# Another written order for a kernel's opening, with products of a zeroed tile and a first weight piece in three parts

## The chip, the core and the metric

The kernel runs on one core of a Trainium2 chip. The metric is device time in microseconds (us) from one launch, and lower is better. A core has TensorE (PE; its weight loads are listed apart, as PEld), VectorE (DVE), ScalarE (ACT), GpSimd (POOL) and SyncE (SP), whose queue issues all DMAs of this kernel. Each engine works through its own instructions in the order in which they stand in the program, and waits there for what the next one needs.

## What is computed

The reference, cut to what matters:

```python
# q, k, v: (4, 8, 576, 64), float32
out_d  = softmax-attention of q, k, v averaged over groups of 4 positions, repeated 4 times
out_l  = softmax-attention over |i - j| < 4 alone
x      = (out_d + out_l) as (2304, 512)
a, b   = x @ w1, x @ w2            # (512, 1024) each
h      = ((a * b) @ w3) @ w_out    # w3 (1024, 1024), w_out (1024, 512)
h2     = h @ w_in                  # (512, 2048)
out    = (h2 * sigmoid(h2)) @ w_out2   # (2048, 512)
```

The arrays come as 64-bit floats and are turned into 32-bit ones on the chip.

## The kernel before

The work is done in three stages that overlap at their edges.

**The opening** is everything up to the first tokens' products with w1 and w2. Three kinds of work are mixed in it. Attention is done in units (one batch and one pair of heads; 16 in all, numbered 0 to 15; the opening does units 0 to 4 and the first part of unit 5). The weights w3 and w_out are multiplied with each other beforehand, so that w3 and w_out need only one product with the tokens later: 64 products of 128x512, named `p` half, pair, number (`p000` to `p137`), on pieces of w3 (names `t`) and w_out (names `o`). And the pieces of w1 and w2 (`w12_0` to `w12_7`) are loaded and turned into a high and a low part. Every piece of a weight goes through a load in two halves (`L...0`, `L...1`), a scaling on ScalarE (`a...`) and three steps on VectorE (`d1`, `d2`, `d3`); a piece of w12 has two more steps (`h` on ScalarE, `l` on VectorE).

In a unit, `Lq`, `Lr`, `Lva`, `Lvb` are its loads; `s` and `sd` the scores on TensorE, `mk`, `ml`, `md`, `rd`, `rl` their masks, maxima and inverse sums on VectorE, `x..` and `n..` exponentials and scalings on ScalarE, `td`, `tl` transposes on TensorE with `cd`, `cl` their copies on ScalarE, `od`, `ol` the sums on TensorE, `pq`, `pv`, `os`, `xf`, `xo` further steps on VectorE, `xh` on ScalarE. `ab` are the products with w1 and w2.

**What sets the order.** The string `OPENING` names every step of the opening, and the program is made by going through it once, so that each engine's order is that of the names that are its own:

```python
    with tc.manual_schedule(engines={T.PE, T.DVE, T.Activation, T.Pool, T.SP}):
        for name in OPENING:
            ops.pop(name)()
```

**Buffers.** The first weight pieces in `KEYS` are loaded into memory lent by later stages (numbers 0 to 3 and 6 to 9 of the list); numbers 4, 5 and all from 10 on share two staging buffers of one tag (`stage(stg, "st")`), so that a load waits until the piece whose buffer it takes has been through its `d3`. Transposes and sums of attention share two PSUM banks, scores two, all 128x512 products four.

**After the opening** the groups `ab`, `y` and the remaining attention units run in slots. `bg_load(n)` loads the 16 pieces of the last two weights in the background, into the same two staging buffers. Then the last stage (`h_unit`, `out_block`) makes the products with w_in and w_out2.

Of the kernel before, what the change touches and what calls it, by code (L numbers as in the profile page):

```python
# [34 lines left out]


OPENING = """
Lwo00 Lwo01 Lq0 Lwt000 Lwt001 Lr0 Lwt010 Lwt011 Lwo10 ao0a d2o0a d1o0a Lwo11 d3o0a ao0b d2o0b
d1o0b d3o0b Lva0 s0 pq0 Lvb0 at00a d2t00a sd0 mk0 ml0 Lq1 at00b d1t00a x00 Lwo20 d3t00a d1t00b
x10 p000 md0 Lwo21 x20 p001 d2t00b d3t00b p002 Lq2 xd0 pv00 rl0 p003 pv10 at01 d2t01 Lwt020 p004  # L40
rd0 n00 d1t01 p005 Lr1 nd0 d3t01 Lwt021 p006 Lwt030 n10 d2o1 td00 n20 td10 p007 cd00 Lwt031 pq1
cd10 tl00 ao1 s1 Lwt100 tl10 cl00 sd1 d1o1 cl10 Lwt101 d3o1 ao2 tl20 od0 cl20 md1 Lwo30 p010 os0
xd1 mk1 p011 ml1 Lq3 ol0 pq2 x01 Lwo31 x11 p012 rd1 pv01 Lwt110 pv11 sd2 nd1 d1o2 d2o2 x21 Lva1
s2 d3o2 p013 at02 Lr2 p014 rl1 d2t02 n01 p015 d1t02 Lvb1 n11 p016 d3t02 n21 Lwt111 p017 d2t03
p020 d2t10 at03 Lww12_30 xf00 p021 xf10 xh00 d1t03 td01 xh10 Lww12_31 td11 d3t03 cd01 p022 cd11
Lwt120 xo00 tl01 ao3 tl11 xo10 p023 d2o3 cl01 Lwt121 d1o3 cl11 p024 Lq4 d3o3 tl21 od1 cl21 md2
p025 os1 p026 xd2 mk2 d2t11 ol1 ml2 rd2 pq3 x02 p027 Lva2 Lvb2 nd2 p030 d2w12_3 sd3 xf01 at10
xf11 pv02 td02 aw12_3 d1t10 td12 s3 d3t10 xh01 xh11 p031 Lq5 x12 d1w12_3 p032 d3w12_3 x22 p033
cd02 d2t12 p034 Lww12_60 hw12_3 Lww12_61 xo01 p035 xo11 wh00 lw12_3 cd12 p036 wh01 wl00 p037
wh02 wl01 p100 wh03 wl02 at11 p101 rl2 wl03 p102 pv12 n02 d1t11 Lr3 aw12_6 p103 d3t11 p104 n12  # L50
d1w12_6 n22 p105 d2w12_6 tl02 d3w12_6 tl12 cl02 p106 cl12 pq4 Lwt130 tl22 od2 Lwt131 cl22 pv03
p107 os2 pv13 p110 at12 md3 Lr4 ol2 mk3 xd3 ml3 d1t12 p111 x03 Lva3 d3t12 Lvb3 sd4 x13 d2t13 s4
Lww12_40 x23 Lww12_41 rd3 xf02 p112 Lq6 nd3 xf12 rl3 p113 md4 n03 pq5 td03 n13 td13 p114 cd03
pv04 cd13 p115 n23 p116 xh02 d2w12_4 aw12_4 tl03 xo02 tl13 cl03 p117 d1w12_4 cl13 xh12 tl23
d3w12_4 xd4 od3 p120 xo12 hw12_6 Lww12_00 os3 p121 Lww12_01 rd4 mk4 hw12_4 lw12_6 p122 at13 p123
lw12_4 cl23 p124 nd4 d1t13 ol3 d3t13 p125 ml4 aw12_0 Lww12_10 d2w12_0 Lww12_11 p126 Lva4 x04
xf03 Lvb4 p127 d1w12_0 xh03 d3w12_0 p130 x14 p131 xo03 x24 Lww12_20 xf13 Lww12_21 p132 pv14
hw12_0 rl4 Lr5 p133 xh13 d2w12_1 aw12_1 p134 lw12_0 p135 n04 d1w12_1 wh10 p136 wh11 d3w12_1 p137
n14 wh12 wl10 td04 Lww12_70 wh13 td14 wl11 Lww12_71 hw12_1 ab000a wl12 ab000b wl13 aw12_2 ab000c
lw12_1 ab001a af00 ab001b n24 d1w12_2 ab001c cd04 d2w12_2 ab010a cd14 cf00 ab010b cc00 ab010c  # L60
aw12_7 d3w12_2 co00 ab011a af01 ab011b xo13 Lww12_50 hw12_2 d1w12_7 ab011c Lww12_51 tl04 d2w12_7
tl14 cl04 sd5 cf01 cl14 cc01 lw12_2 tl24 co01 od4 cl24 s5 d3w12_7 ab020a Lq7 os4 ab020b hw12_7
md5 ab020c mk5 aw12_5 ab021a lw12_7 ab021b af02 ab021c ml5 xd5 ab030a d1w12_5 ab030b x05 cf02
ab030c cc02 x15 rd5 ab031a d2w12_5 co02 ab031b d3w12_5 af03 ab031c nd5 ab040a cf03 x25 ab040b
cc03 ab040c co03 hw12_5 rl5 ab041a ab041b af04 lw12_5 n05 ab041c ol4 n15 cf04 n25 cc04 ab050a
co04 Lva5 xf04 ab050b xf14 Lvb5 xh04 ab050c xh14 xo04 ab051a af05 xo14 ab051b ab051c ab060a cf05
ab060b cc05 ab060c co05 ab061a af06 ab061b ab061c ab070a cf06 ab070b cc06 ab070c co06 ab071a
af07 ab071b ab071c ab100a cf07 ab100b cc07 ab100c co07 ab101a af10 ab101b ab101c cf10 cc10 co10
""".split()


# [1067 lines left out]
```

## Time and profile before

| | |
|---|---|
| median of 3 runs | 860.12 us (859.17 to 861.5) |
| the profiled execution's own time | 860.39 us |
| its span, first to last instruction | 858.6 us |
| TensorE busy | 832.3 us, 97% of the span |
| VectorE, ScalarE, GpSimd busy | 490.9, 304.8, 266.0 us |
| mean granted TensorE clock | 0.995 |

The profile is of one execution. Busy time of TensorE counts a product from its start to its modelled end, so a busy TensorE need not be one at full speed. A time without a name in what follows is counted from the span's start. A product with 32-bit operands has two records.

### The profile page before, as it was taken

What the parts mean: (1) busy time and instruction counts of PE and PEld (TensorE: products, weight loads), DVE (VectorE), ACT (ScalarE), POOL (GpSimd) and SP (SyncE); (2) the same over time, 40 slices, a digit from 0 to 9 for tenths busy, and PEclk for the clock granted to TensorE, in tenths of its full rate; (3) what the DMA queues carried; (4) which work ended last, traced back from release to release, by engine and by line L of the source; (5) the groups of instructions that cost most, each with busy time, mean ns of one, the idle gap of its engine ahead of it and who ended that gap; (6) DMA issues with size and microseconds to landing.
All of it is one profiled execution on the core that took longest, in us unless ns stands there. A gap on an engine that the chain in (4) does not pass through costs nothing.

```text
span 858.6 us, 17384 instructions
## 1 busy us (share of the span) xinstructions
PE 832.3 (97%) x7104; PEld 738.1 (86%) x7104; DVE 490.9 (57%) x831; ACT 304.8 (36%) x880; POOL 266.0 (31%) x214
## 2 busy tenths in 40 slices
PE   5999999999999999999999999999999999999996
PEld 3544688999999999999999899899998999989985
DVE  6898984476564746446954444446544447534433
ACT  5777854454434553543322111122211123211111
POOL 3000132353533545131443133235232434222210
PEclk9999999999999999999999999999999999999999
DMA  9976663364546462426960675362662432822403
GB/s 322 347 250 195 202 201 99 126 223 158 206 139 220 152 212 82 179 89 237 349 269 23 251 264 214 134 220 87 178 227 86 129 128 86 235 97 99 158 2 74
DMA packets 39728, 149.16 MB, mean 174 GB/s; under 512 B 4448, under 2 KB 11616, under 8 KB 33504
## 3 DMA queue, kind: packets, MB, share of 16 engines
q1 hardware_dynamic: 39648, 148.05, 50.8%
q8 instruction: 56, 0.92, 0.4%
q14 instruction: 24, 0.20, 0.1%
HBM read 115.52 MB, written 32.51 MB: 172 GB/s over the span
## 4 chain that ended last, share of the span: by engine, by line
PE 88%; DVE 5%; DMA 4%; ACT 1%; issue 1%; SPq 0%
PE o L957 23%; PE ab L619 23%; PE h L1033 20%; PE y L684 12%; PE wp L571 3%; DMA st<-w 2%; PE ol L456 2%; DMA qk<-qk 1%; PE tl L404 1%; PE sd L332 1%; PE td L382 1%; PE s L357 1%; PE od L434 1%; ACT band L304 1%; DMA lent<-wo 0%
## 5 line engine op out<-in xcount | busy, mean ns | idle before, releaser
L957 PE MATMUL o<-wo,g 128*128 128x512 f32 x864 | 221.4, 393 | 0.0
L957 PEld LDWEIGHTS o<-wo,g 128*128 128x128 f32 x864 | 160.7, 188 | 25.3
L1004 POOL TENSOR_TENSOR g<-sg,g 128x768 fp32r<-128x768 f32 x46 | 84.9, 1845 | 250.1 <-DVE g L1002 242.3
L1033 PE MATMUL h<-yc,wcb 128*128 128x384 f32 x576 | 116.1, 337 | 0.0
L684 PE MATMUL y<-c,w_wC 128*128 128x320 f32 (+1 forms) x768 | 111.1, 301 | 0.0
L619 PE MATMUL ab<-x,w_wB 128*128 128x320 f32 (+1 forms) x768 | 108.9, 296 | 1.3 <-DVE w_wB L249 1.3
L1033 PEld LDWEIGHTS h<-yc,wcb 128*128 128x128 f32 x576 | 103.3, 188 | 7.7
L659 POOL TENSOR_TENSOR c<-cf,c 128x320 fp32r<-128x320 f32 (+1 forms) x64 | 74.1, 1158 | 107.2 <-DVE c L654 102.4
L619 PE MATMUL ab<-x,w_wA 128*128 128x320 f32 (+1 forms) x768 | 106.2, 296 | 0.1
L684 PEld LDWEIGHTS y<-c,w_wC 128*128 128x128 f32 x768 | 104.2, 191 | 1.3 <-issue 1.0
L619 PEld LDWEIGHTS ab<-x,w_wB 128*128 128x128 f32 x768 | 102.2, 188 | 2.6 <-DVE w_wB L249 1.6
L619 PEld LDWEIGHTS ab<-x,w_wA 128*128 128x128 f32 x768 | 102.1, 188 | 0.9 <-DVE w_wA L249 0.3
L996 ACT ACTIVATE sg<-cf 128x768 f32<-128x768 f32 x24 | 20.3, 847 | 184.7 <-DVE cf L1021 184.7
L1033 PE MATMUL h<-yc,wca 128*128 128x384 f32 x432 | 83.4, 336 | 1.4 <-DVE cg L1021 1.4
L1033 PEld LDWEIGHTS h<-yc,wca 128*128 128x128 f32 x432 | 76.5, 188 | 5.5 <-DVE cg L1021 1.7
L635 DVE TENSOR_TENSOR cf<-ab,af 128x320 f32<-128x320 f32 (+1 forms) x64 | 29.0, 454 | 63.7 <-PE ab L619 51.5
L571 PE MATMUL wp<-w_wo,w_w 128*128 128x512 f32 x128 | 62.9, 634 | 0.9 <-DVE w_w L178 0.9
L418 POOL TENSOR_TENSOR vr<-vr 72x512 f32<-72x512 f32 x11 | 15.7, 1432 | 118.3 <-DMA vr<-vr 118.2
L996 ACT ACTIVATE sg<-cg 128x768 f32<-128x768 f32 x24 | 20.3, 847 | 88.4 <-DVE cg L1021 88.4
L1021 DVE TENSOR_TENSOR u<-h,u 128x384 f32<-128x384 f32 x48 | 26.6, 553 | 40.1 <-PE h L1033 39.9
L571 PEld LDWEIGHTS wp<-w_wo,w_w 128*128 128x128 f32 x128 | 24.2, 201 | 26.9 <-issue 23.7
L304 ACT ACTIVATE band<-band,sml 128x38 f32<-128x38 f32 x144 | 45.0, 318 | 5.5 <-DVE sml L373 2.9
(111 smaller groups left out, 991.8 us busy)
## 6 DMA issues: line engine op xcount, KB each, us to landing
wcb<-wsd SPq DMA_DIRECT2D x24, 1024.0 KB
wca<-wsd SPq DMA_DIRECT2D x24, 768.0 KB
sw<-wb SPq DMA_DIRECT2D x32, 512.0 KB
qk<-qk SPq DMA_DIRECT2D x16, 579.0 KB
st<-w SPq DMA_DIRECT2D x16, 512.0 KB
wsd<-res SPq DMA_DIRECT2D x8, 1024.0 KB
wod<-res SPq DMA_DIRECT2D x8, 1024.0 KB
wo<-wod SPq DMA_DIRECT2D x8, 1024.0 KB
```

The costliest lines, as they stand in the source:

```text
L304: nc.scalar.activation(E[:, j, :], src[:, j, :], AF.Exp, bias=z[:, j:j + 1], scale=scale, accum_out=z[:, NQB + j:NQB + j + 1],)
L456: nc.tensor.matmul(acc[h][r, c0:c0 + QW], lhsT=v[k, sub, c, r], rhs=ET[k, c, q0:q0 + QW], start=True, stop=True,)
L571: nc.tensor.matmul(wp_ps[half, j], lhsT=w3v[:, k, j * P:(j + 1) * P], rhs=wov[:, k, :], start=(gp == 0 and k == 0), stop=(gp == 3 and k == 1),
L619: nc.tensor.matmul(acc[:, :N], lhsT=wv[:, i, w, kk, :], rhs=X[b, h, kk][:, j, :], start=(n == 0), stop=(n == 11),)
L635: nc.vector.tensor_tensor(out=cf, in0=C.pop(("ab", b, h, m, 1))[:, :N], in1=C.pop(("af", b, h, m)), op=ALU.mult)
L659: mark(nc.gpsimd.tensor_tensor(out=c[:, 1], in0=C.pop(("cf", b, h, m)), in1=c[:, 0].bitcast(F32), op=ALU.subtract))
L684: nc.tensor.matmul(acc[:, :N], lhsT=WP[kf // 2][:, i, kf % 2, ec * P:(ec + 1) * P], rhs=c[:, j, :], start=(kf == 0 and n == 0), stop=(kf = ...
L957: nc.tensor.matmul(acc, lhsT=g[:, a, j * P:(j + 1) * P], rhs=w[:, b, half, :], start=(p == 0 and half == 0 and n == 0), stop=(p == 7 and h ...
L996: nc.scalar.activation(sg, c, AF.Sigmoid)
L1004: e.tensor_tensor(out=g[:, 1], in0=sg, in1=g[:, 0].bitcast(F32), op=ALU.subtract)
L1021: nc.vector.tensor_tensor(out=out_, in0=in0, in1=in1, op=op)
L1033: nc.tensor.matmul(acc, lhsT=wc[w][:, a, c, kt * P:(kt + 1) * P], rhs=y[:, b, kt, :], start=(n == 0), stop=(n == 5),)
```

## The change

The order in `OPENING` is another one throughout, and so is the list `KEYS`: the first piece of w3 is now loaded and decoded ahead of the first of w_out, in three parts instead of two (256, 256 and 512 columns), and the pieces of w12 come in the order 0, 2, 3, 1, 5, 4, 6, 7 instead of 3, 6, 4, 0, 1, 2, 7, 5. A zeroed tile of 128x320 is made by VectorE; nine products of 128 of its columns with 288 of its columns stand at the very start of TensorE's program, and two more (`z0`, `z1`) behind `sd0`; nothing reads their result. `bg_load(1)` is planned six slots later.

```diff
@@
+NWARM = 9
@@
 OPENING = """
-Lwo00 Lwo01 Lq0 Lwt000 Lwt001 Lr0 Lwt010 Lwt011 Lwo10 ao0a d2o0a d1o0a Lwo11 d3o0a ao0b d2o0b
+Lwt000 Lwt001 Lwt002 Lq0 Lwo00 Lwo01 Lwt010 Lwt011 at00a d2t00a Lwo10 d1t00a Lwo11 at00b d3t00a
...
@@
+    zero = att.tile([P, TOK[0]], F32, tag="xf", name="zero")
+    nc.vector.memset(zero, 0.0)
+    spare = mm_tile("spare")
+
+    def idle_product():
+        nc.tensor.matmul(
+            spare[:, :288], lhsT=zero[:, :P], rhs=zero[:, :288], start=True, stop=True
+        )
+
+    for _ in range(NWARM):
+        idle_product()
@@
-    def weight_ops(n, key, split):
+    def weight_ops(n, key, cuts):
...
+        whole = not cuts
+        cuts = cuts or [(0, 0, 512), (1, 0, 512)]
+
+        def load(k):
+            t, c0, c1 = cuts[k]
...
-                raw[key][:, t].rearrange("p n w -> p (n w)"), w_source(key, t).bitcast(I32)
+                raw[key][:, t, c0:c1].rearrange("p n w -> p (n w)"),
+                w_source(key, t)[:, c0:c1].bitcast(I32),
...
-        for x in (range(2) if split else (None,)):
-            part(x)
+        if whole:
+            part(slice(0, 1024), "")
+        else:
+            for (t, c0, c1), suffix in zip(cuts, "abcd"):
+                part(slice(512 * t + c0, 512 * t + c1), suffix)
@@
-    SPLIT = (('wo', 0), ('w3', (0, 0)))
+    CUTS = {('wo', 0): [(0, 0, 512), (1, 0, 512)], ('w3', (0, 0)): [(0, 0, 256), (0, 256, 512), (1, 0, 512)]}
@@
+    for k in range(2):
+        op(f"z{k}", idle_product)
@@
-    at(NSTATIC, lambda: bg_load(1))
+    at(NSTATIC + 6, lambda: bg_load(1))
```

How the order moves instructions is seen at three places. The first is the start of TensorE's program (`s` and `sd` are unit 0's scores, `wp` the products `p000` on). Before:

```order
L357 MATMUL s_150<-qk_126 32x38 x36
L332 MATMUL sd_193<-qkd_187 64x144 x6
L571 MATMUL wp_0_219<-w_wo,w_w_190 128x512
L571 MATMUL wp_1_229<-w_wo,w_w_190 128x512
L571 MATMUL wp_2_233<-w_wo,w_w_190 128x512
```

And of the change:

```order
L126 MATMUL spare<-zero 128x288 x9
L376 MATMUL s_166<-qk_139 32x38 x36
L351 MATMUL sd_210<-qkd_203 64x144 x6
L126 MATMUL spare<-zero 128x288 x2
L592 MATMUL wp_0_236<-w_wo,w_w_147 128x512
L592 MATMUL wp_1_244<-w_wo,w_w_147 128x512
L592 MATMUL wp_2_254<-w_wo,w_w_147 128x512
```

Nothing of the old order has moved here; eleven products stand in between.

The second place is ScalarE's program around unit 3's transposes. The copies to `ET` are `cl03`, `cl13` and, last, `cl23`; `dec<-st` is the scaling of a w12 piece straight from its staging buffer (w12_4 before, w12_3 in the change). Before:

```order
L482 CAST x_0_992<-xf_0_947 128x320
L161 ACTIVATE dec<-st 128x1024
L411 COPY ET_997<-tl_0_998 102x256
L411 COPY ET_997<-tl_2_1002 102x256
L482 CAST x_1_1009<-xf_1_955 128x256
L304 ACTIVATE Ed_1014,smd<-sd_891,smd 128x144 x3
L246 CAST w_wA<-dec 128x1024 x2
L161 ACTIVATE w_w_1040<-st 128x1024
L411 COPY ET_997<-tl_4_1011 38x128
```

And of the change, with unit 4's transposed scores behind it (`cd04`, `cd14` are the copies to `EdT_1188`):

```order
L323 ACTIVATE Ed_1022,smd<-sd_847,smd 128x144 x3
L174 ACTIVATE dec<-st 128x1024
L430 COPY ET_1026<-tl_0_1027 102x256
L430 COPY ET_1026<-tl_2_1030 102x256
L338 ACTIVATE Ed_1022<-Ed_1022,smd 128x144 x3
L430 COPY ET_1026<-tl_4_1046 38x128
L265 CAST w_wB<-dec 128x1024
L174 ACTIVATE w_w_1069<-st 128x1024
L323 ACTIVATE band,sml<-band,sml 128x38 x9
L174 ACTIVATE dec<-st 128x1024
L338 ACTIVATE band<-band,sml 128x38 x9
L409 COPY EdT_1188<-td_0_1189 72x2x128
```

The copies still stand behind a scaling that waits for a load, but of another piece; and the next such scaling (w12_1) has unit 4's scalings and copies behind it.

The third place is SyncE's queue where the staging buffers are taken in turn. In the change `st<-w3t` is first the third-to-last piece of w3 (t11), then, behind the loads of units 2 and 5, the piece t12; `st<-w` between them is w12_2:

```order
L221 DMA st<-w3t 128x1024
L221 DMA st<-w 128x1024 x2
L296 DMA vw_700<-vw 40x1280
L296 DMA vw_700<-vw 40x2x512
L302 DMA vr_734<-vr 80x1024
L289 DMA qk_811<-qk 128x1158
L221 DMA st<-w3t 128x1024 x2
L221 DMA st<-w 128x1024 x2
L296 DMA vw_909<-vw 40x1280
```

Before, t11 lay in lent memory and t12 was the second staged piece from there on:

```order
L204 DMA lent<-w3t 128x1024
L204 DMA st<-w 128x1024 x2
L204 DMA st<-w3t 128x1024 x2
L270 DMA qk_572<-qk 128x1158
L277 DMA vw_647<-vw 40x1280
```

So t11, t12 and t13 now pass through the two staging buffers in turn with w12 pieces between them.

## Rows read from the trace of the kernel before

**Rows 1.** The page: span, TensorE's busy time, the instruction queue (packets, MB, share)

```profile
span 858.6 us, 17384 instructions
...
PE 832.3 (97%) x7104; PEld 738.1 (86%) x7104; DVE 490.9 (57%) x831; ACT 304.8 (36%) x880; POOL 266.0 (31%) x214
...
q8 instruction: 56, 0.92, 0.4%
```

**Rows 2.** Waits of PE, whole span: total us, times, longest

```profile
PE s L357 <- DMA qk<-qk: 7.4, 1, 7.4
PE ol L456 <- issue: 3.1, 2, 2.1
PE tl L404 <- ACT ET L411: 1.9, 1, 1.9
PE s L357 <- issue: 1.5, 1, 1.5
PE h L1033 <- DVE cg L1021: 1.4, 1, 1.4
PE ab L619 <- DVE w_wB L249: 1.3, 1, 1.3
PE sd L332 <- DVE qkd L290: 1.1, 1, 1.1
PE wp L571 <- DVE w_w L178: 0.9, 1, 0.9
```

**Rows 3.** Windows: busy of each engine (x records), clock, DMA share, GB/s

```profile
0.00:50.00 50.00, 38.06 (x484) 20.99 (x484) 38.20 (x73) 31.28 (x115) 6.92 (x20) 1.00 0.98 335
50.00:75.00 25.00, 25.00 (x306) 13.42 (x306) 24.58 (x45) 21.24 (x75) 0.00 (x0) 1.00 0.65 208
...
165.00:473.00 308.00, 307.93 (x3551) 296.00 (x3550) 182.52 (x330) 132.95 (x428) 121.17 (x112) 1.00 0.51 179
```

**Rows 4.** Timeline of PE, first 40 us: start, us, form, records

```profile
7.38 1.36 PE L357 MATMUL s<-qk 64*32 64x38 f32 x72 [7.38 <-DMA qk<-qk]
...
12.45 8.30 PE L571 MATMUL wp<-w_wo,w_w 128*128 128x512 f32 x14 [0.86 <-DVE w_w L178]
...
25.30 1.98 PE L571 MATMUL wp<-w_wo,w_w 128*128 128x512 f32 x4
...
32.92 6.28 PE L571 MATMUL wp<-w_wo,w_w 128*128 128x512 f32 x14
```

**Rows 5.** Timeline of DVE from 20 us: unit 1's sum, then w_out's second piece

```profile
20.74 1.35 DVE L290 TENSOR_REDUCE qkd<-qk 128x288 f32<-128x1152 f32 x1 [1.68 <-DMA qk<-qk]
23.01 0.69 DVE L166 TENSOR_SCALAR w_wo<-w_wo 128x1024 f32<-128x1024 f32 x1 [0.92 <-ACT w_wo L161]
23.74 1.23 DVE L178 SCALAR_TENSOR_TENSOR w_wo<-w_wo,lent 128x1024 int32<-128x1024 int32 x1
```

**Rows 6.** Timelines of SP, ACT and PE, 71 to 88 us

```profile
71.61 1.77 SPq L204 DMA_DIRECT2D st<-w  x2
...
78.96 1.17 ACT L161 ACTIVATE dec<-st 128x1024 f32<-128x1024 f32 x1 [2.30 <-DMA st<-w]
...
80.44 0.29 PE L404 MATMUL tl<-ident,band 128*38 128x128 f32 x1 [1.90 <-ACT ET L411]
...
81.34 6.25 PE L571 MATMUL wp<-w_wo,w_w 128*128 128x512 f32 x10
```

**Rows 7.** Timeline of PE behind the opening

```profile
147.91 0.53 PE L456 MATMUL ol<-ET,vw 38*64 38x32 f32 x15 [2.09 <-issue]
```

**Rows 8.** Windows in which the granted clock (third number from the end) fell

```profile
82.00:84.50 2.50, 2.50 (x4) 1.01 (x3) 2.47 (x8) 2.50 (x4) 0.00 (x0) 0.50 0.44 115
...
149.00:151.00 2.00, 2.00 (x12) 2.00 (x11) 0.59 (x3) 0.77 (x2) 1.23 (x2) 0.67 0.60 148
```

**Rows 9.** Timelines: DVE's d3 of t11; PE's products p125 to p137

```profile
61.69 1.23 DVE L178 SCALAR_TENSOR_TENSOR w_w<-w_w,lent 128x1024 int32<-128x1024 int32 x1
...
88.81 9.71 PE L571 MATMUL wp<-w_wo,w_w 128*128 128x512 f32 x22
```

More of the change, by code (lines that the diff above doesn't have):

```diff
@@ L37 @@
 OPENING = """
-Lwo00 Lwo01 Lq0 Lwt000 Lwt001 Lr0 Lwt010 Lwt011 Lwo10 ao0a d2o0a d1o0a Lwo11 d3o0a ao0b d2o0b
[L39 to L67, printed above, removed]
@@ L68 @@
-af07 ab071b ab071c ab100a cf07 ab100b cc07 ab100c co07 ab101a af10 ab101b ab101c cf10 cc10 co10
+Lwt000 Lwt001 Lwt002 Lq0 Lwo00 Lwo01 Lwt010 Lwt011 at00a d2t00a Lwo10 d1t00a Lwo11 at00b d3t00a
+d2t00b d1t00b d3t00b Lva0 at00c d2t00c d1t00c d3t00c Lvb0 s0 pq0 Lr0 ao0a d2o0a sd0 z0 z1 mk0
+ml0 Lq1 ao0b d1o0a d3o0a x00 md0 p000 Lwo20 x10 d1o0b p001 d2o0b xd0 d3o0b Lq2 p002 d2t01 x20
+p003 rd0 Lwo21 at01 rl0 p004 p005 nd0 d1t01 Lwt020 p006 d3t01 Lwt021 n00 Lwo30 td00 n10 d2o1
+td10 Lwo31 p007 n20 pv00 ao1 pv10 Lwt030 pq1 s1 cd00 cd10 tl00 tl10 d1o1 Lr1 cl00 sd1 cl10 d3o1
@@ new lines @@
+tl20 od0 Lwt031 cl20 md1 p010 os0 xd1 pq2 p011 Lq3 ao2 p012 d2o2 Lwt100 p013 rd1 mk1 nd1 p014
+d1o2 Lwt101 d3o2 sd2 at02 d2t02 s2 Lww12_00 md2 p015 d1t02 p016 Lww12_01 d3t02 ao3 p017 ml1 ol0
+Lq4 d1o3 x01 Lwt110 p020 pv01 x11 pv11 p021 d2o3 Lva1 x21 d3o3 p022 at03 p023 rl1 Lr2 d2t03 p024
+n01 d1t03 n11 p025 d3t03 Lvb1 n21 p026 pq3 p027 Lwt111 p030 d2t10 at10 xf00 p031 Lww12_20 xf10
+xh00 td01 d1t10 xh10 td11 cd01 d3t10 Lww12_21 p032 cd11 xd2 tl01 d2w12_0 tl11 p033 xo00 cl01 rd2
+cl11 tl21 xo10 aw12_0 p034 mk2 ml2 od1 cl21 wh00 d1w12_0 p035 nd2 wl00 p036 os1 wh01 d3w12_0
@@ new lines @@
+p037 x02 ol1 wl01 wh02 wh03 pv02 p100 x12 wl02 Lva2 Lvb2 wl03 p101 x22 xf01 p102 xf11 hw12_0 rl2
+td02 pv12 td12 n02 d2t11 Lr3 p103 n12 lw12_0 p104 n22 d2w12_2 sd3 xh01 xh11 xo01 cd02 s3 xo11
+cd12 md3 tl02 at11 Lq5 tl12 pq4 p105 cl02 p106 cl12 aw12_2 d1t11 tl22 d3t11 od2 cl22 xd3 p107
+os2 Lwt120 d1w12_2 p110 Lwt121 d3w12_2 sd4 rd3 ol2 Lww12_30 hw12_2 mk3 Lww12_31 ml3 nd3 p111
+lw12_2 Lva3 Lvb3 x03 p112 xf02 p113 x13 xf12 pv03 td03 x23 d2t12 td13 p114 pv13 at12 md4 Lr4
+p115 rl3 xh02 d1t12 s4 xh12 n03 d3t12 p116 Lq6 n13 p117 xo02 Lwt130 n23 xo12 Lwt131 p120 d2w12_3
@@ new lines @@
+cd03 cd13 pq5 p121 xd4 tl03 tl13 pv04 aw12_3 p122 rd4 p123 cl03 d1w12_3 cl13 nd4 tl23 d3w12_3
+od3 p124 cl23 os3 Lww12_10 hw12_3 mk4 p125 Lww12_11 ml4 at13 p126 lw12_3 p127 x04 d1t13 ol3 x14
+d2t13 d3t13 x24 sd5 Lva4 Lvb4 pv14 s5 Lww12_50 rl4 Lr5 xf03 aw12_1 p130 Lq7 d2w12_1 Lww12_51
+td04 xf13 n04 p131 d1w12_1 n14 d3w12_1 td14 n24 p132 md5 cd04 p133 Lww12_40 cd14 Lww12_41 hw12_1
+tl04 tl14 p134 cl04 lw12_1 cl14 tl24 xh03 p135 wh10 xo03 cl24 od4 mk5 wh11 wl10 p136 xh13 aw12_5
+wl11 p137 os4 xo13 wh12 ab000a d1w12_5 wh13 ab000b wl12 xd5 ab000c wl13 ab001a af00 d2w12_5
@@ new lines @@
+ab001b aw12_4 ab001c d3w12_5 ab010a ab010b cf00 Lww12_60 hw12_5 ab010c cc00 Lww12_61 d1w12_4
+ab011a co00 af01 ab011b lw12_5 ab011c ab020a d2w12_4 ab020b cf01 ab020c cc01 ab021a d3w12_4 af02
+co01 ab021b ab021c rd5 Lww12_70 hw12_4 d2w12_6 ab030a Lww12_71 cf02 ab030b aw12_6 cc02 ab030c
+lw12_4 co02 ab031a nd5 ab031b d1w12_6 af03 ab031c d3w12_6 ab040a ab040b cf03 ab040c hw12_6 cc03
+ab041a ml5 co03 ab041b af04 lw12_6 aw12_7 ab041c ab050a x05 cf04 ab050b cc04 ab050c x15 d1w12_7
+co04 ab051a d2w12_7 af05 ab051b x25 d3w12_7 ab051c ab060a cf05 ab060b hw12_7 cc05 ab060c rl5
@@ L69 @@
+ab061a co05 af06 lw12_7 ab061b n05 ab061c n15 ol4 cf06 n25 cc06 ab070a co06 Lva5 xf04 ab070b
+Lvb5 xf14 xh04 ab070c xh14 xo04 ab071a af07 xo14 ab071b ab071c ab100a cf07 ab100b cc07 ab100c
+ab101a co07 af10 ab101b ab101c cf10 cc10 co10
 """.split()
@@ L194, in weight_ops @@
         hold = {}
-        def load(t):
+        whole = not cuts
+        cuts = cuts or [(0, 0, 512), (1, 0, 512)]
+        def load(k):
+            t, c0, c1 = cuts[k]
             if key not in raw:
@@ L204, in load @@
             nc.sync.dma_start(
-                raw[key][:, t].rearrange("p n w -> p (n w)"), w_source(key, t).bitcast(I32)
-            )
-        for t in range(2):
-            op(f"L{'w'}{name}{t}", lambda t=t: load(t))
+                raw[key][:, t, c0:c1].rearrange("p n w -> p (n w)"),
+                w_source(key, t)[:, c0:c1].bitcast(I32),
+            )
+        for k in range(len(cuts)):
+            op(f"Lw{name}{k}", lambda k=k: load(k))
         def place():
@@ L223, in place, with part @@
             )
-        def part(x):
+        def part(r, suffix):
             def step(k):
-                r = slice(0, 1024) if x is None else slice(512 * x, 512 * x + 512)
                 st = raw[key].rearrange("p t n w -> p (t n) w")[:, r]
@@ L255, in weight_ops @@
         op("l" + name, rest)
-    KEYS = [('wo', 0), ('w3', (0, 0)), ('w3', (1, 0)), ('wo', 1), ('wo', 2), ('w3', (2, 0)), ('w3', (3, 0)), ('w3', (0, 1)), ('wo', 3), ('w3', (1, 1)), ('w12', 3), ('w3', (2, 1)), ('w12', 6), ('w12', 4), ('w3', (3, 1)), ('w12', 0), ('w12', 1), ('w12', 2), ('w12', 7), ('w12', 5)]
-    SPLIT = (('wo', 0), ('w3', (0, 0)))
+    KEYS = [('w3', (0, 0)), ('wo', 0), ('w3', (1, 0)), ('wo', 1), ('wo', 2), ('w3', (2, 0)), ('wo', 3), ('w3', (3, 0)), ('w3', (0, 1)), ('w12', 0), ('w3', (1, 1)), ('w12', 2), ('w3', (2, 1)), ('w12', 3), ('w3', (3, 1)), ('w12', 1), ('w12', 5), ('w12', 4), ('w12', 6), ('w12', 7)]
+    CUTS = {('wo', 0): [(0, 0, 512), (1, 0, 512)], ('w3', (0, 0)): [(0, 0, 256), (0, 256, 512), (1, 0, 512)]}
     for n, key in enumerate(KEYS):
-        weight_ops(n, key, key in SPLIT)
+        weight_ops(n, key, CUTS.get(key))
     A = {}
```

1 line of the change is left out of this document (removed).

## The prediction

> **What bounds the kernel now.** I read the page first [rows 1]: TensorE is busy 97% of an 858.6 us span, so the change can take away only TensorE's idle time, and products that are slow. Then the waits of TensorE [rows 2]: 18.6 us have a cause there; most of the other 7.7 of the 26.3 idle us are behind the last product. Then windows by stage [rows 3]: from 165 to 473 us TensorE is busy 307.93 of 308 us. The change ends before that stage, so each microsecond won or lost ahead of 165 us should come out whole at the end. The prediction is therefore a sum over the opening's stalls, place by place, against the execution's own 860.39 us.
>
> What limits the opening changes on the way. In the first 50 us the DMA engines are 98% busy at 335 GB/s [rows 3]: here data arrive as fast as they can, and the order of the loads is all that can be chosen. From 50 to 75 us TensorE has no idle time and VectorE works 24.58 of 25 us. After that TensorE stops at single places.
>
> **The start.** TensorE first waits 7.38 us for unit 0's q and k, then does its first fourteen product records in 8.30 us; the same fourteen take 6.28 us from 32.92 on [rows 4]. So the first products lose 2.0 us to a half-speed clock (1.2 of 2.4 GHz; the clock column of the windows shows 1.00 there, so it is the durations that tell). The nine products of zeros fill the first wait. A record of 512 columns takes 0.449 us at speed (6.28/14), one of 288 columns by proportion 0.25, or 0.50 at half speed: eighteen records last 4.5 to 9.0 us. If they start at about 1 us (an estimate; TensorE has nothing ahead of them but VectorE's clearing of the tile), they end at 5.5 to 10.0 us. The late end would hold unit 0's scores back by 2.6 us, the early one costs nothing, and in return the first products may run at speed.
>
> Neither matters much, because something later sets the pace. The second weight pair's first product (p010) starts at 25.30 us [rows 4]. Its w_out piece is decoded by VectorE behind the pooling of unit 1's q and k, which waits until 20.74 us for their load, and then by 0.92 us for ScalarE's scaling [rows 5]. In the change the same pieces stand ahead of that load in the queue, so the same bytes; at 335 GB/s it lands at 20.7 us again. Behind it VectorE now needs 1.35 + 0.69 + 1.23 = 3.3 us without the wait for ScalarE, whose scaling of that piece now stands ahead of unit 0's transposed copies instead of behind them. That makes 24.0 us: **-1.3 us**. The 3 us of idle and half-speed time that the warm products could save end up as a wait for that load. Where this cover is gone the start gives up to 2.0 us more; where the scaling is late again, nothing.
>
> The first piece of w3 in three parts costs one more transfer and three more small VectorE steps. I count it as 0: the DMA engines are busy whatever the number of pieces. Bounds: 0, or half of the 1.77 us that SyncE's queue took for two issues [rows 6]. The Trainium skill speaks against small pieces: its page DMA: Bandwidth & Descriptors, Rules for kernel authors, asks for at least 1 MiB per transfer, and its anatomy of one DMA gives a fixed cost of about 2.0 us for each (fitted on another path than SyncE's); if that lay bare here, the estimate would be 2.0 us more and the sum 857.2. No run here shows a transfer by itself; 335 GB/s with half-pieces and 98% busy engines speaks for hidden.
>
> **Three waits without a named cause** ("issue"): 1.5 us in unit 2's scores, 3.1 - 2.1 = 1.0 us in one of the units' sums, both inside the first 50 us, and 2.1 us at 147.91 [rows 2, 7]. All three are in the small products, where 72 records take 1.36 us [rows 4]. The page counts 56 packets and 0.92 MB on the instruction queue [rows 1], 16 KB each, so TensorE's program itself is fetched in pieces over busy DMA engines; I take these waits for late fetches, which is an inference. The new order shifts what stands in each piece. It doesn't remove small products or free the DMA engines in the first 50 us, so waits of this kind will come back at other places: I take 1.0 of the 2.5 us, between 0 and 2.5: **-1.5 us**. The one at 147.91 comes from the steps behind the opening, whose order is as before, and the shift by eleven products can't be followed there: **0**.
>
> **The stall at 78 us** is the clearest. SyncE issues the load of w12_4 at 71.61, when a staging buffer comes free; it lands at 78.96, 7.35 us later. ScalarE stands at its scaling until then, with two copies of unit 3's transposes behind it, and TensorE's last transpose waits 1.90 us for a buffer that those copies free [rows 6]. The clock then falls to its lower level (0.50 from 82.00 to 84.50 [rows 8]): ten records take 6.25 us instead of 10 x 0.449 = 4.49, another 1.8. In the change the scaling ahead of these copies is that of w12_3. Its buffer comes free when w12_2 is decoded, and between that and this scaling stand all of unit 3's maxima and exponentials and the decoding of t12. So it should be there: **-3.7 us**.
>
> **The stall at 109 us** is TensorE waiting 1.3 us for the low part of w12_2 [rows 2]. In the change w12_0 and w12_2 are the first two w12 pieces; the ones used late (4, 6, 7) are decoded last, beside products that take as long: **-1.3 us**.
>
> **New waits.** VectorE is nearly full from 50 to 75 us, and t12, whose load had long been there, now passes through the staging buffers. After t11's d3 (it ends at 62.92 [rows 9]) comes a load of 7.35, then scaling, d1 and d3 of 1.17 + 0.69 + 1.23 = 3.1 us [rows 5, 6], and the same again for t13. So even with t11 no earlier than before, p130 can start at 62.92 + 2 x 10.45 = 83.8. Before, three products of two records ahead of it, it started at 88.81 + 6 x 0.441 = 91.5 [rows 9]. This chain allows up to 7.7 us of gain there, and the three terms ahead of it (1.3, 1.5, 3.7) ask for 6.5. It is a close fit with little left for a slow load, and the scaling of w12_1 now has unit 4's copies behind it. For this I add **+2.0 us**, between 0 and 5.5 (a whole second stall of the kind at 78 us, 3.7, and a slow stretch, 1.8). The clock fell after idle stretches of 1.9 and 2.1 us; TensorE's waits for q and k at the start may do the same: half of 1.8, **+0.9 us**.
>
> The later `bg_load(1)` I count as 0: its buffer is not free sooner, and TensorE has no wait for that weight in the stage from 165 us [rows 3].
>
> **Sum:** -1.3 - 1.5 - 3.7 - 1.3 + 2.0 + 0.9 = -4.9, so 860.39 becomes 855.5. The median of the runs shown is 0.27 lower than this execution; for a median I say 855.2.
>
> **Rivals.**
> - *All the stalls go.* No new wait, no late fetch in the first 50 us: -1.3 - 2.5 - 3.7 - 1.3 = -8.8, 851.3; with the wait at 147.91 and its slow stretch gone (2.1 + 1.8) 847.4. For it: each has a cause of its own that the order removes. Against it: the chain of t11, t12, t13 has 1 us to spare. Chance 0.20.
> - *The stall moves.* A scaling again stands in ScalarE's order ahead of copies that TensorE needs, likeliest w12_1's, whose buffer comes free only with w12_3's d3. Then 3.7 + 1.8 stand for the 2.0 + 0.9: -2.3, 857.8; with both unnamed waits back (1.0 more) 858.8. For it: the same 7.35 us load and the same two buffers. Against it: w12_1's load starts with all of t13's decoding ahead of its scaling. Chance 0.19.
> - *The staging chain becomes the bound,* on the other side. If the loads of t12 and t13, behind those of units 2 to 6 in the queue, take longer than 7.35 us, each microsecond counts twice at p130. At 11.2 us each the gain there is gone (62.92 + 2 x 14.3 = 91.5); at 13.4 us each p130 is at 95.9, and with 109's 1.3 us off that is +3.1, 863.2. Against it: from 50 to 75 us the DMA engines are 65% busy. Chance 0.08.
>
> **How the numbers follow.** The sum's own case, 852.5 to 857.5, has 0.53. The range shall leave out no more than 0.2: below 850 is about half of the first rival (0.10), above 860 the last and little of the second (0.09); so 850 to 860. A measurement of this kernel tells from no change about 0.3%, 2.6 us. Faster by more than that: the sum's case and the first rival, 0.73. Within it: the moved stall, 0.19. Slower: 0.08.
>
> **What would show it.** In the changed kernel's profile: p010's first record at about 24 us, and unit 1's pooling again waiting for its load until about 20.7; fourteen records of the first products in 6.3 us if the warm products work; no wait of a transpose on a copy to ET, no fall of the clock at 80 us; no wait of `ab` products on w12; p130 between 83.8 and 87. I am wrong in the start if p010 moves by over 2 us, in the chain if p130 waits for VectorE's d3 of t13, and in the whole if the stage from 165 us on doesn't pass the gain through.

## The result, and the profile after

The changed kernel takes 848.26 us (median of 4 runs, 847.63 to 850.36) against 860.81 us (859.17 to 862.05) for the kernel before in the same session: a ratio of 0.9863, with a 95% interval of 0.9842 to 0.9885. It is faster, as forecast, but by 12.5 us and not by 5: the time lies under the range of 850 to 860.

The page of the changed kernel, the rows that answer to [rows 1]:

```profile
span 846.4 us, 17434 instructions
...
PE 832.3 (98%) x7126; PEld 738.2 (87%) x7126; DVE 493.7 (58%) x835; ACT 304.0 (36%) x881; POOL 265.8 (31%) x214
...
q8 instruction: 56, 0.92, 0.5%
```

The span is 12.2 us shorter with the same 832.3 us of busy TensorE, although 7.6 us of that is now products of zeros (6.41 and 1.24 in the timeline below). So real products must have become quicker by about as much, and the rest is idle time that is gone. What idle time is left is in the waits of TensorE (total us, times, longest):

```profile
PE s L376 <- DMA qk<-qk: 1.6, 2, 1.2
PE h L1054 <- DVE cg L1042: 1.4, 1, 1.4
PE spare L126 <- DVE zero L122: 1.3, 1, 1.3
PE sd L351 <- DVE qkd L309: 1.0, 1, 1.0
PE tl L423 <- ACT ET L430: 0.6, 1, 0.6
PE wp L592 <- DVE w_wo L191: 0.4, 1, 0.4
```

Beside [rows 2], every row that read "issue" is missing, and so is the wait of `ab`. The transposes' wait is 0.6 us in place of 1.9. The windows by stage, with the clock third from the end:

```profile
0.00:50.00 50.00, 45.64 (x447) 25.17 (x448) 42.96 (x81) 33.89 (x115) 6.68 (x20) 1.00 0.98 332
50.00:75.00 25.00, 25.00 (x375) 14.05 (x374) 23.46 (x44) 22.59 (x92) 0.00 (x0) 1.00 0.69 207
75.00:110.00 35.00, 34.35 (x318) 24.44 (x317) 31.47 (x52) 24.37 (x69) 8.12 (x6) 1.00 0.71 226
110.00:165.00 55.00, 54.98 (x732) 51.00 (x731) 38.55 (x71) 31.29 (x121) 19.19 (x22) 1.00 0.50 164
165.00:460.00 295.00, 294.96 (x3382) 283.70 (x3377) 171.72 (x310) 123.33 (x389) 115.16 (x106) 1.00 0.51 180
```

Against [rows 3]: the DMA engines are as busy as before in the first 50 us, TensorE hardly stops from 110 to 460 us, the clock does not fall in these stretches, and the stage from 165 us on runs without a gap, as before. The timeline of TensorE (start, us, form, records, the wait ahead in brackets) at the places of which the prediction speaks:

```profile
1.29 6.41 PE L126 MATMUL spare<-zero 128*128 128x288 f32 x18 [1.29 <-DVE zero L122]
8.06 0.85 PE L376 MATMUL s<-qk 64*32 64x38 f32 x72 [0.35 <-DMA qk<-qk]
...
10.82 1.24 PE L126 MATMUL spare<-zero 128*128 128x288 f32 x4
12.50 6.28 PE L592 MATMUL wp<-w_wo,w_w 128*128 128x512 f32 x14 [0.44 <-DVE w_wo L191]
...
24.74 4.56 PE L592 MATMUL wp<-w_wo,w_w 128*128 128x512 f32 x10
...
84.91 1.13 PE L592 MATMUL wp<-w_wo,w_w 128*128 128x512 f32 x2
...
91.23 0.29 PE L423 MATMUL tl<-ident,band 128*38 128x128 f32 x1 [0.57 <-ACT ET L430]
...
136.29 1.35 PE L475 MATMUL ol<-ET,vw 38*64 38x32 f32 x72
137.58 5.55 PE L705 MATMUL y<-c,w_wC 128*128 128x320 f32 x36
```

Where the first fourteen product records took 8.30 us in [rows 4] they take 6.28. The row at 24.74 is p010 (25.30 before), that at 84.91 is p130 (about 91.5 before). Unit 5's sums at 136.29 run through; before, the wait of 2.09 us in [rows 7] split them, and the 36 `y` records behind them took 7.08 us and not 5.55.

Rows of the kernel before that the next lines use (scores, sums and `y` records around the unnamed waits):

```profile
30.44 0.70 PE L357 MATMUL s<-qk 64*32 64x38 f32 x55
...
45.46 1.50 PE L456 MATMUL ol<-ET,vw 38*64 38x32 f32 x66
...
144.77 1.06 PE L456 MATMUL ol<-ET,vw 38*64 38x32 f32 x57
...
148.37 7.08 PE L684 MATMUL y<-c,w_wC 128*128 128x320 f32 x36
```

A ledger up to the end of those 36 records, from these rows and those of before: unit 0's scores start 0.7 us later. Waits behind that start: 9.8 us before (the sum of [rows 2] without q and k and without `h`), 3.2 now: -6.6. The scores, coarse scores and first products of unit 0 at full speed (1.36 + 1.71 + 8.30 us before, 0.85 + 0.95 + 6.28 now): -3.3. The ten records behind the stall at 80 us, 6.25 us before [rows 6] and 10 x 0.449 at speed: -1.8. The `y` records: -1.5. The small products on both sides of the three unnamed waits, which together take 1.05, 1.91 and 1.59 us before and 0.85, 1.35 and 1.35 now: -1.0. Two more products of zeros: +1.2. Together -12.3, beside -12.2 in the spans. So the gain is nowhere but ahead of these records' end (143 us in the changed kernel), and about half of it is waits, the rest mostly products that ran slowly.

Two more views of the changed kernel serve the steps below. VectorE's pooling of unit 1 and the decoding of w_out's second piece ([rows 5] before):

```profile
21.47 1.35 DVE L309 TENSOR_REDUCE qkd<-qk 128x288 f32<-128x1152 f32 x1
22.74 0.68 DVE L179 TENSOR_SCALAR w_wo<-w_wo 128x1024 f32<-128x1024 f32 x1
23.46 1.22 DVE L191 SCALAR_TENSOR_TENSOR w_wo<-w_wo,lent 128x1024 int32<-128x1024 int32 x1
```

And ScalarE's scaling of w12_3 ahead of unit 3's copies, which stood there 2.30 us for a load in [rows 6] and now finds its data there:

```profile
74.44 1.16 ACT L174 ACTIVATE dec<-st 128x1024 f32<-128x1024 f32 x1
75.88 0.65 ACT L430 COPY ET<-tl 102x256 f32<-102x256 f32 x2 [0.28 <-PE tl L423]
```

### The profile page after: what moved, and what is told of

Same layout as the page of the kernel before. It is cut to its first block, busy times and chain, and to the rows that moved or that the text cites. A ratio compares the mean times of both kernels' runs of the same rounds, so it can differ in the third digit from the quotient of the medians.

```text
span 846.4 us, 17434 instructions
## 1 busy us (share of the span) xinstructions
PE 832.3 (98%) x7126; PEld 738.2 (87%) x7126; DVE 493.7 (58%) x835; ACT 304.0 (36%) x881; POOL 265.8 (31%) x214
## 4 chain that ended last, share of the span: by engine, by line
PE 90%; DMA 5%; DVE 4%; issue 0%; ACT 0%; SPq 0%; ACTq 0%
PE o L978 24%; PE ab L640 23%; PE h L1054 21%; PE y L705 12%; PE wp L592 3%; DMA vr<-vr 2%; PE ol L475 2%; DMA st<-w 2%; PE sd L351 1%; PE tl L423 1%; PE s L376 1%; PE td L401 1%; PE od L453 1%; DMA lent<-wo 1%; DVE dec L191 1%
## 5 line engine op out<-in xcount | busy, mean ns | idle before, releaser
L592 PE MATMUL wp<-w_wo,w_w 128*128 128x512 f32 x128 | 60.1, 602 | 0.5 <-DVE w_wo L191 0.4
L650 ACT COPY af<-ab 128x320 f32<-128x320 f32 (+1 forms) x64 | 25.4, 397 | 56.4 <-PE ab L640 56.4
```

The costliest lines, as they stand in the source:

```text
L592: nc.tensor.matmul(wp_ps[half, j], lhsT=w3v[:, k, j * P:(j + 1) * P], rhs=wov[:, k, :], start=(gp == 0 and k == 0), stop=(gp == 3 and k == 1),
L650: mark(nc.scalar.copy(af, C.pop(("ab", b, h, m, 0))[:, :N]))
```

## The experiments

Three theories stood at the start. **A**: waits of TensorE without a named cause are late fetches of its own program, which comes in pieces over the same DMA engines; the eleven products move every later instruction against the pieces, and so take these waits away, whatever the products compute. **B**: the products act through the clock (they keep TensorE at speed). **C**: the gain is the order's alone, and the products give nothing. Times are compared by the ratio to the kernel before in the same session; 0.1% is 0.86 us. The ratio is worked out from all runs and differs by up to 0.2% from that of the two medians, so it, with its interval, decides. A timeline or a list of waits is of one execution, which can lie some us off the median.

### The products, one by one

**no_products**: the changed kernel without the zeroed tile and its products.

```diff
-NWARM = 9
+NWARM = 0
...
-... sd0 z0 z1 mk0
+... sd0 mk0
```

> The changed kernel without its eleven products of zeros, all else as in it (848.3 us). Theory A, late fetches of TensorE's own program: the products' 44 instructions moved the places at which a piece of the program has to be there, so without them the wait of about 2.1 us in unit 5's sums and the half-speed stretch of 1.8 us behind it come back, and perhaps one wait of 1.0 to 1.5 us in the first 50 us: 852 to 853.5. Theory B, the products pay by the clock of the first real products: these take 8.3 instead of 6.3 us, 850.3, and no wait behind the opening. Theory C, they do nothing for the time: 848.3.

851.96 us, 0.9888 (0.9860 to 0.9916). By this time alone A, B and C can't be told apart, but the trace has a wait of A's kind:

```profile
139.34 0.48 PE L464 MATMUL ol<-ET,vw 38*64 38x32 f32 x14 [0.80 <-issue]
139.75 7.08 PE L692 MATMUL y<-c,w_wC 128*128 128x320 f32 x36
```

An unnamed wait stands again in unit 5's sums, and the `y` records behind it are slow again (7.08 us). The two early unnamed waits don't come back: the order by itself has moved TensorE's instructions too.

**tiny_products**: the changed kernel with products of 8 columns instead of 288, as many instructions.

```diff
-            spare[:, :288], lhsT=zero[:, :P], rhs=zero[:, :288], start=True, stop=True
+            spare[:, :8], lhsT=zero[:, :P], rhs=zero[:, :8], start=True, stop=True
```

> The changed kernel with the same eleven products made 8 columns wide instead of 288, so that the count of instructions stays and TensorE's work in its early waits goes. Theory A: no wait in unit 5's sums, the first products slow (8.3 us) but hidden by the load of unit 1's q and k, 848.3 to 849.0. Theory B: about 850.3, as without the products. Theory C: 848.3.

849.87 us, 0.9858 (0.9830 to 0.9886): no difference from the changed kernel that these intervals tell. No unnamed wait. The first fourteen records take 8.39 us, as slowly as before the change, and p010 starts 1.3 us later than with wide products. So the wide products do what they look made for, 2 us of clock at the start, but if it is worth something at the end it is less than some 3 us.

**before_products**: the kernel before, with nothing but the eleven products.

```diff
-... sd0 mk0 ml0 Lq1
+... sd0 z0 z1 mk0 ml0 Lq1
...
+    for _ in range(9):
+        idle_product()
```

> The kernel before (860.8 us) with the eleven products at the same places, nothing else changed. Theory A: the wait and slow stretch behind the opening (2.1 + 1.8) go, of the two unnamed waits in the first 50 us the one in unit 1's sums (1.0) goes and the one in unit 2's scores (1.5) stays, the start gains 0.3 because w_out's second piece is decoded no earlier: about 855.6. Theory B: only the start gains, about 2.0: 858.8. Theory C: 860.8.

856.36 us, 0.9949 (0.9930 to 0.9968): -4.4 us, for products whose result nobody reads. The waits of TensorE in it:

```profile
PE ol L467 <- DMA vw<-vw: 2.0, 1, 2.0
PE ab L632 <- DVE w_wB L260: 1.8, 1, 1.8
...
PE tl L415 <- ACT ET L422: 0.9, 1, 0.9
```

All three unnamed waits of [rows 2], 4.6 us, are gone, also the one in unit 2's scores, which I had expected to stay. Part of them comes back: unit 1's sums wait 2.0 us for a load, and `ab` 1.8 us in place of 1.3.

**before_tiny_products**: the same with 8 columns.

> The kernel before with the eleven products 8 columns wide: the count of instructions moves, the clock at the start does not. Theory A: nearly all of the gain of the wide products, 855.9 or so, with the first products still slow. Theory B: 860.8, no gain. Theory C: 860.8.

856.33 us, 0.9949 (0.9929 to 0.9970). The same gain with the first fourteen records at 8.41 us. B is out: what pays here is not the clock.

**before_64_small**, **before_32_small**: if what pays is the number of the instructions, then a whole piece of them must bring the time back. A product is four instructions (two records, each with a weight load), and the page's 2 x 7126 records over 56 packets are 254 to a packet; so 64 products, 256 instructions, should be one 16 KB piece. The edit is shown against the run above; with 32 products the loop has 30.

```diff
-            spare[:, :8], lhsT=zero[:, :P], rhs=zero[:, :8], start=True, stop=True
+            spare[:32, :8], lhsT=zero[:32, :32], rhs=zero[:32, :8], start=True, stop=True
...
-    for _ in range(9):
+    for _ in range(62):
```

> The kernel before with 64 small products (32 x 32 x 8 columns, of the zeroed tile) in place of the eleven: 62 ahead of everything, two behind unit 0's coarse scores. 64 products are 256 instructions of TensorE, exactly one 16 KB piece of its program, so each later instruction stands again where it stood within its piece. Theory A (late fetches; what counts is where the pieces begin): the unnamed waits come back in unit 2's scores (about 32 us), in a unit's sums (about 48 us) and in unit 5's sums (about 148 us), with the slow stretch behind the last, and the time is 860 to 861 (+-1). Theory B (any early products, or the tile and the clearing that come with them, keep the waits away): 856.4, no unnamed wait. If the 64 take longer than the 7.4 us wait for q and k, up to 2 us of that can show in both.

> The same with 32 small products, half a piece of the program. Theory A: the pieces begin 128 instructions earlier than before; waits without a named cause of 0.5 to 2.5 us may stand at other places, none where they were at 32, 48 and 148 us; time anywhere between 856 and 860.5. Theory B: 856.4 and no unnamed wait.

With 64: 860.02 us, 0.9999 (0.9974 to 1.0024). With 32: 856.95 us, 0.9958 (0.9938 to 0.9979). Eleven products give 4.4 us, 32 give 3.6, 64 give nothing. The two largest waits of TensorE with 64:

```profile
PE tl L415 <- ACT ET L422: 2.7, 1, 2.7
PE s L368 <- issue: 2.4, 1, 2.4
```

And its timeline around the second of them:

```profile
30.13 0.69 PE L368 MATMUL s<-qk 64*32 64x38 f32 x55
33.20 0.48 PE L368 MATMUL s<-qk 64*32 64x38 f32 x17 [2.38 <-issue]
33.62 9.15 PE L584 MATMUL wp<-w_wo,w_w 128*128 128x512 f32 x14
```

Unit 2's scores stop again behind the 55th of their 72 records, exactly where they did in the kernel before (55 records, a wait, 17 records). The other two unnamed waits did not come back in this profiled execution, although A had expected them too. That its time is nearly the old one comes, in this execution, mostly from this one wait: it is longer than before (2.38 for 1.50 us), and behind it the clock is at its lower level from 32.7 to 39.4 us, so that fourteen records take 9.15 us, which took 6.28 in [rows 4]. So the run bears A out in the place of the wait and in the time, but not in all three waits. With 32 one of 0.4 us stood at a new place, 187 us. The record of the instruction queue's packets shows the mechanism (fetch start, when TensorE went on; us):

```
kernel before:    30.20 -> 32.64   45.52 -> 47.95   145.36 -> 147.91
with 64 products: 30.87 -> 33.20
```

Each time TensorE goes on 2.3 to 2.6 us after a fetch of 16 KB begins. (A packet does not name the engine whose program it brings; that these bring TensorE's is read from their times.) The places of the stops say the same. Number TensorE's instructions in each trace as they start (products, weight loads, and the few that only handle semaphores). In the kernel before, 705, 962 and 3009 of them start ahead of the product behind the wait, with 64 products 961, and each number is 193 or 194 past a multiple of 256. So it is for all 18 unnamed waits of 0.3 us or more in the traces of this case; all stand in `s` or `ol`, the smallest products, and end 2.3 to 2.8 us after a fetch began. **Theory A is shown** for the products' part.

One detail is other than A has it. With the eleven products (before_products) the same numbers, 705, 961 and 3009, still fall in unit 2's scores, unit 1's sums and unit 5's sums, and TensorE passes them at 29.20, 45.76 and 142.18 us without a stop. The last fetches ahead of the first and the third began at 26.18 and 137.57, 3.0 and 4.6 us earlier. With 64 products TensorE reaches the places of the other two waits at 50.05 and 149.01 us, 2.6 and 2.4 us after the fetches at 47.41 and 146.62, so the pieces came just in time. What counts is thus how long before TensorE reaches a piece its fetch has begun, and the place decides through that.

**before_late_tiny**: eleven tiny products at the `ab` products' wait at 109 us of the kernel before, into unused columns of their bank. Only what comes later is shifted.

```diff
+        if (b, h, m, w, q) == (0, 0, 2, 0, 0):
+            for _ in range(11):
+                nc.tensor.matmul(
+                    acc[:, 400:408], lhsT=ident, rhs=ident[:, :8], start=True, stop=True
+                )
```

> The kernel before with eleven tiny products (8 columns, into unused columns of a bank) put into TensorE's wait for w12_2's low part at 109 us, so that only what stands behind shifts by 44 instructions and clock and order of the opening stay. Late fetches as the cause: the waits in the first 50 us stay (1.5 and 1.0), the wait in unit 5's sums and its slow stretch go, less up to 1 us that the tiny products take beyond the wait: 857 to 858. Otherwise: 860.8 or a little more, with the wait at about 148 us still there.

859.08 us, 0.9984 (0.9961 to 1.0006): not told from nothing. The timeline:

```profile
83.53 0.40 PE L404 MATMUL tl<-ident,band 128*38 128x128 f32 x1 [2.41 <-ACT ET L411]
...
85.02 7.18 PE L571 MATMUL wp<-w_wo,w_w 128*128 128x512 f32 x10
...
113.72 2.62 PE L619 MATMUL ab<-ident 128*128 128x8 f32 x22
...
150.00 1.35 PE L456 MATMUL ol<-ET,vw 38*64 38x32 f32 x72
151.29 5.55 PE L689 MATMUL y<-c,w_wC 128*128 128x320 f32 x36
```

The late wait and its slow stretch are gone (2.1 + 1.5 us), while the early unnamed waits, ahead of the shift, stay, as A says. But the products take 2.6 us for themselves where the wait that they fill was 1.3. What is left is 2.3, where 2.8 to 3.8 had been expected, and the interval reaches from 3.4 to -0.5.

**bg_back**: the changed kernel with the second background load at its old step.

```diff
-    at(NSTATIC + 6, lambda: bg_load(1))
+    at(NSTATIC, lambda: bg_load(1))
```

> The changed kernel with the second background load back at its old step (the same as the first one's). My term for it was 0: 848.3 +-1, and the stage behind 165 us as before. Rival: the later load is what lets the program's fetch at 132 us through ahead of the 1 MB background load; then a wait of about 2 us without a named cause comes back in unit 5's sums or the products behind them, with a slow stretch: 850 to 852.

849.25 us, 0.9857 (0.9823 to 0.9890), no unnamed wait: this edit is worth nothing that could be measured, and isn't what keeps the wait in unit 5's sums away.

### The order

**before_copies_first**: the kernel before, with two of unit 3's copies ahead of the scaling of w12_4.

```diff
-... d2w12_4 aw12_4 tl03 xo02 tl13 cl03 p117 d1w12_4 cl13
+... d2w12_4 tl03 xo02 tl13 cl03 p117 cl13 aw12_4 d1w12_4
```

> The kernel before with one edit of the order: on ScalarE the two copies of unit 3's transposes stand ahead of the scaling of w12_4 instead of behind it, so TensorE's last transpose there no longer waits for that load. My sum's theory: the whole place is saved, 1.9 of wait and 1.8 of slow stretch, 857.1 from 860.8. Rival: VectorE's decoding of w12_4 still waits for the same load, so the pieces behind it come no earlier, and what is saved at 80 us is given back in the wait for w12_2's low part, which grows from 1.3 to about 5 us: 860 to 861.

860.11 us, 0.9987 (0.9964 to 1.0009). The wait at 80 us, which I had called the clearest and put at 3.7 us, is gone, but the time can't be told from the old one, and its interval (3.1 us faster to 0.8 slower) leaves 3.7 out. TensorE's timeline shows where part of it went:

```profile
98.93 7.30 PE L619 MATMUL ab<-x,w_wB 128*128 128x320 f32 x48 [1.11 <-DVE w_wC L585]
...
111.29 7.16 PE L619 MATMUL ab<-x,w_wB 128*128 128x320 f32 x47 [1.75 <-DVE w_wB L249]
...
123.98 10.67 PE L619 MATMUL ab<-x,w_wA 128*128 128x320 f32 x71 [0.38 <-DVE w_wA L249]
```

3.2 us of waits of `ab`, where there were 1.3. VectorE's work for w12 did not get any earlier: the step on `w_wB` that ends the wait at 111 us starts at 110.03, in the kernel before at 109.58. So TensorE only came to it sooner. The profile doesn't give the whole sum: this execution was 2.5 us late ahead of the place (the products next to it start at 79.98 us, in the kernel before at 77.51), behind unnamed waits of 0.6 and 2.4 us and a stretch at the lower clock.

**before_pieces**: the kernel before, its places for w12 decoding the pieces in the changed kernel's order (the names in `OPENING` likewise).

```diff
-    KEYS = [... 3 ... 6 ... 4 ... 0 ... 1 ... 2 ... 7 ... 5]   # the numbers of its w12 pieces
+    KEYS = [... 0 ... 2 ... 3 ... 1 ... 5 ... 4 ... 6 ... 7]
```

> The kernel before with its opening as it is, except that the eight places which decode pieces of w12 take them in the changed kernel's order (0, 2, 3, 1, 5, 4, 6, 7 in place of 3, 6, 4, 0, 1, 2, 7, 5). My term for the stall at 109 us by itself: the 1.3 us wait of the ab products goes, and nothing else changes: 859.1 (-1.3, +-1 about 860.4). Rival: the wait is for whatever piece comes at that place, and another wait of the ab products takes over: 860.4.

859.14 us, 0.9987 (0.9961 to 1.0013). The wait of `ab` at 109 us is gone from the trace, as expected; the time fits the expected -1.3 and also nothing. The transposes' wait at 80 us is 0.7 us in this execution, with the same order of the copies, and the unnamed waits are 5.6 us; so these two may differ between executions as well as by the edit.

**before_pieces_copies**: both.

> The same, and the two copies of unit 3's transposes ahead of the scaling of the third w12 piece, as in the run that gave nothing by itself. If that run gave nothing because the saving was caught by the ab products' waits for w12, it comes out now: 859.1 - 1.9 - 1.8 = 855.4, with no wait of a transpose at 80 us and none of ab. Rival: the saving is caught elsewhere (by the products' results, w_wC, which cost 1.1 us there): 858 to 860.

857.86 us, 0.9969 (0.9948 to 0.9991): -2.7 (-4.5 to -0.8) of the 5.0 that the two terms have together. Alone the two edits had -1.1 each by the same measure, each within some 2 us, so these times don't show that one needs the other. In the trace there is no wait for w12 any more, but two others catch part of the saving, as the rival said, though its 858 to 860 was a little high:

```profile
87.23 1.25 PE L456 MATMUL ol<-ET,vw 38*64 38x32 f32 x68 [0.70 <-ACT ET L411]
...
99.80 7.30 PE L619 MATMUL ab<-x,w_wB 128*128 128x320 f32 x48 [1.03 <-DVE w_wC L585]
```

**before_pieces_copies_products**: these and the eleven products.

> The same with the eleven products of the changed kernel as well. If the terms add up, 855.4 less the 4.1 us that the products gave in the kernel before: 851.3; what remains to the changed kernel's 848.3 is then the start and the loads' order. Rival: with fewer waits the chain of w12's loads holds, 854 to 856.

853.31 us, 0.9926 (0.9898 to 0.9955): -6.4, between the two forecasts. With the same three edits the changed kernel is 5.4 us faster still (0.9863). Its waits:

```profile
PE s L368 <- DMA qk<-qk: 2.1, 1, 2.1
PE sd L343 <- DVE qkd L301: 1.8, 2, 1.6
PE ol L467 <- DMA vw<-vw: 1.4, 1, 1.4
...
PE ab L632 <- DVE w_wC L598: 1.1, 1, 1.1
PE wp L584 <- DVE w_w L189: 0.8, 2, 0.4
PE ol L467 <- ACT ET L422: 0.7, 1, 0.7
```

With the 1.3 us for the zeroed tile and 0.3 of transposes these are 9.5 us, and the changed kernel has 4.9 (its rows above without `h`): 4.6 us. From 50 to 75 us its clock is 0.95 instead of 1.00, 1.25 us. That is 5.9 of the 6.1 us between the two spans (852.5 and 846.4). So by these two executions the rest of the order's gain is mostly loads and decoded data that come in time: unit 1's q and k, the values (`vw`) for the sums, the first decoded pieces and the first results of `p`. This last part is read from the traces and not shown by a run; none took the loads' order alone.

### Two edits to the changed kernel's opening

**two_parts**: w3's first piece in two parts (the names in `OPENING` follow).

```diff
-('w3', (0, 0)): [(0, 0, 256), (0, 256, 512), (1, 0, 512)]
+('w3', (0, 0)): [(0, 0, 512), (1, 0, 512)]
```

> The changed kernel with the first piece of w3 in two parts as before, all else as in it. If three parts cost nothing (my sum): 848.3 to 848.8. If the extra transfer delays what is queued behind it: unit 1's q and k land up to 0.7 us earlier (20.7 instead of 21.45 us) and the time falls by about as much, 847.6.

848.76 us, 0.9874 (0.9841 to 0.9907): not told from the changed kernel. In the profiled execution, 2.1 us above the median, unit 1's scores wait 2.8 us for their q and k, the clock falls behind that wait, p010 is at 27.62 and not 24.74, and the span is 2.6 us longer (849.0): there the late start came out nearly whole at the end. As the median isn't later, this is put down to that execution and not to the edit.

**q1_first**: unit 1's q and k loaded ahead of unit 0's values.

```diff
-... at00b d3t00a d2t00b d1t00b d3t00b Lva0 ... Lvb0 s0 pq0 Lr0 ... Lq1 ...
+... at00b d3t00a d2t00b d1t00b d3t00b ... s0 pq0 ... Lq1 Lva0 Lvb0 Lr0 ...
```

> The changed kernel with the load of unit 1's q and k ahead of unit 0's three loads of v, and its pooling ahead of unit 0's sums of v on VectorE. If that load sets the pace of the start: TensorE's wait of 1.2 us at 20 us goes and p010 starts 0.9 to 1.2 us earlier, 847.2 from 848.3. If something later sets it (v for unit 0's sums, or w_out's second piece): no change.

850.09 us, 0.9886 (0.9854 to 0.9919): a miss for the first, and the rival is what happened. Unit 1's wait of 1.2 us goes, but unit 0's coarse sums (`od`) wait 2.4 us for the values instead, and p010 is at 26.18. In this stretch, with the DMA engines 98% busy, what one load gained another lost.

## Why the prediction was too small

**The step that failed is the one on the three waits without a named cause.** Its mechanism, late fetches of TensorE's program, was right, and the runs show it. What was wrong is what I made of it: that "waits of this kind will come back at other places", so that I took 1.0 of 2.5 us back, and that the one at 147.91 stays, worth 0. All three went, and with the last its slow stretch: 4.6 + 1.5 = 6.1 us of TensorE's time, where the sum has 1.5; the small products around them, which ran slower, make it 7.1. Of the shifts tried in the kernel before, eleven products lost all three, 32 left 0.4 us at another place, and only a whole piece brought the time back. Three shifts are few, but in them "gone" was the better guess than "elsewhere". I also wrote that the shift by eleven products can't be followed at 147.91. It can, as its 44 instructions are a sixth of a piece, but it would have left the stop in unit 5's sums; what I lacked is that the fetch then begins 4.6 us ahead. What sets the start of a fetch no run here shows.

**The stall at 78 us**: right for the changed kernel, where the scaling finds its data and the clock holds. But as a term by itself, -3.7, it was wrong: alone it gave nothing that could be measured, 3.1 us at most, and the `ab` products behind it waited for 1.9 us more. That it pays with the terms beside it fits the changed kernel, but the runs that combine them don't settle it. I had read what releases the stall, not what waits 20 us later.

**The stall at 109 us**, -1.3: the wait went, in the change and in before_pieces; its own worth couldn't be told from nothing.

**The start**, -1.3 at p010: measured -0.56. The chain was as I had it, pooling and then 3.3 us of VectorE (21.47 to 24.74), but the load landed at about 21.5 and not 20.7. The fast first products work (6.28 us), and what they are worth at the end is below what could be measured, which fits my argument that a load sets the pace there but doesn't show it.

**w3's first piece in three parts**, 0, and **bg_load(1)**, 0: neither can be told from 0 (two_parts, bg_back). The Trainium skill's page DMA: Bandwidth & Descriptors gives a fixed cost of about 2.0 us for each transfer (Anatomy of one DMA; fitted on another path than SyncE's). My estimate from it, 2.0 us more for the additional transfer, does not show here: 0.9863 with it, 0.9874 without, though intervals of this width could hide 2 us.

**The staging chain**: right. p130 starts at 84.91 us, inside 83.8 to 87, and nothing waits there. **New waits**, +2.0: 0.6 us measured, one transpose at 91.23 behind ScalarE's cast of a w12 piece. **Clock**, +0.9: 0, as it does not fall ahead of 460 us.

Of the 7 us by which the sum was short, the unnamed waits have 4.6 (5.6 with the small products around them), the new waits 1.4 and the clock 0.9; the start gave 0.7 less than its term. My first rival, "all the stalls go", with the wait at 147.91 among them (847.4), is what happened. I had given it 0.20, on the ground that the chain of t11, t12 and t13 had only 1 us to spare; 1 us was enough.

## What to carry to other kernels

A wait of TensorE that the profile gives no cause for, amid small products and busy DMA engines, was here a wait for the next 16 KB piece of its program. Anything that adds or removes instructions ahead of such a wait can move it or cure it, so part of a measured gain may have nothing to do with what was edited. A few useless instructions, and a whole piece of them, help to tell which part that is.

A stall is worth its length only if nothing behind it is late by itself (the stall at 80 us, 3.7 us on paper, measured 1.1 alone, and 3.1 at the most): before crediting it, look at the next places where the same engine meets the engines that did not get faster.
